# The last matrix of a decode block: other cuts of its transfer, fewer wide products

## The chip, the cores and the metric

The kernel runs on one core of a Trainium2 chip. The metric is the device time of one execution in microseconds; runs are compared by their median. Everything is in float32.

## What is computed

One decode step of a transformer block for a batch of four tokens: an adaptive layer norm conditioned on `c`, attention over a window of 2048 cached positions (32 query heads, 8 key and value heads), a second adaptive layer norm, and a gated feed-forward net. The change touches the last product of the feed-forward net alone. Its part of the reference:

```python
def _B_ref(x, w1, w3, w2):
    gate = jnp.einsum("bsd,df->bsf", x, w1)
    up = jnp.einsum("bsd,df->bsf", x, w3)
    h = _silu(gate) * up
    out = jnp.einsum("bsf,fd->bsd", h, w2)
    return out

...
h = _layernorm(x, axis=-1) * (1 + cb) + sb
x = x + gb * _B_ref(h, B_w1, B_w3, B_w2)
```

`w1` and `w3` are 512 x 1792, `w2` is 1792 x 512, and there are four tokens.

## The kernel before

The kernel reads about 100 MB once and in a fixed order: modulation weights, `wq`, the key and value blocks of eight groups, `wo`, `w1`, `w3`, `w2`. All of it goes through one large tile, `ring`, whose parts are loaded again when their last reader is done. SyncE issues nearly all of the transfers. The program is written out as one list of operations; `Program` works out the waits from the tiles that the operations touch. Each engine carries out its own operations in the order of the list. `do.mark()` splits the list in two parts with semaphores of their own: when all engines have passed the mark, GpSimd clears the semaphores of the first part.

The feed-forward net ends the kernel. `ffn_in` (line 431) multiplies the normed tokens `h2T` with `w1`, then with `w3`, into `s_ps[0]` and `s_ps[1]`; ScalarE copies the result out, TensorE transposes it, and VectorE makes the hidden values, `hidT` (line 459). `hidT` holds 14 chunks of 128 hidden features, and `w2` has 14 chunks of 128 rows by 512 columns to match (256 KB a chunk).

`w2` is loaded at line 412 in four pieces, one transfer each, cut at `W2_CUTS`, which counts chunks: 8, 3, 2 and 1. The transfers are issued one behind another on SyncE's queue, behind that of `w3`. A product waits for the piece that holds its columns.

Two forms of product are used for a chunk:

- **Wide** (lines 466 to 468): one product of 512 columns for a chunk, into one of four strips of 32 partitions of `part` (`s_ps[3]`). Four chunks go to four strips, the next four are added to them. So each strip ends as a partial sum over its own chunks, and the four strips have to be added together. ScalarE copies `part` to `work` (line 469), and TensorE adds the strips by a product of `work` with `sames`, a matrix of ones and zeros.
- **Narrow** (`add_rows`, line 471): eight products of 64 columns for a chunk, one for each of four strips `j` and two halves `s`. They put the output into `y_ps` (`s_ps[2]`) in its final place: strip `j` holds columns `j * 128` to `j * 128 + 127`, and the two halves `s` of these lie in different rows of the strip. No addition of strips is needed. `add_rows(sames, work, ...)` takes the partial sums of the wide products into `y_ps` by the same route.

A float32 product appears as two matmul instructions in the profile, each with a weight load of its own.

The order on TensorE's queue is: chunks 0 to 7 wide; chunks 8, 9, 10 narrow; `sames` by `work`; chunks 11 and 12 narrow; the mark; chunk 13 narrow. VectorE then multiplies `y_ps` with the gate and adds the residual (lines 484 and 485), and SyncE writes the result out (line 486). The input layout on the host (`_layout`, line 490) puts the weights in the order in which the chunks are read; `edge` holds the last two chunks.

Of the kernel before, what the change touches and what calls it, by code (L numbers as in the profile page):

```python
# [8 lines left out]
B, D, HQ, G, SK, DH, W, FF = 4, 512, 32, 8, 8192, 128, 2048, 1792  # L9
P = 128  # L10
# [2 lines left out]
NC = 4  # L13
NF = FF // P
BLOCK = FF // 4
W2_CUTS = [0, 8, 11, 13, 14]
GUESTS = 240
GUEST_AT = [(0, 0, 12), (12, 0, 12), (24, 0, 8), (64, 0, 12), (76, 0, 12), (84, 4, 12)]
EPS = 1e-5
# [128 lines left out]
def block_kernel(nc, w_mod_a, wq, guests, kv_in, wo_mod, last_k_wo, last_v, wo, w1, w3, w2, out):  # L148
# [5 lines left out]
    do = Program(nc)  # L154

    def sb(name, *shape):
        return nc.alloc_sbuf_tensor(name, (P, *shape), F32).ap()
# [16 lines left out]
    def load(dst, src, cuts=(0, 1), queue="sync"):  # L174
        step = src.shape[1] // cuts[-1]
        for lo, hi in zip(cuts[:-1], cuts[1:]):
            do(queue, "dma_start", dst[:, lo * step : hi * step], src[:, lo * step : hi * step])
        return dst[:, : src.shape[1]]
# [7 lines left out]
    first = load(slots[0], w_mod_a)  # L186
# [22 lines left out]
    hidT = sb("hidT", NF, 36)  # L209
# [11 lines left out]
    sames = sb("same", 36)  # L221
# [83 lines left out]
    work = sb("work", 512)  # L305
    for half in range(2):
        qp = s_ps[half]
        for k in range(4):
            for i in range(4):
                at = ((half * 4 + i) * 4 + k) * 512  # L310
                n = min(512, 16384 - GUESTS - at)
# [28 lines left out]
    def heads_out(g):  # L340

        otp = bank()[:, : R * B]
        if g < G - 1:
            do("tensor", "matmul", otp, o_sum, pick, start=True, stop=True)
        else:
            for c in range(NC):
                do("tensor", "matmul", otp, work[:, c * P : (c + 1) * P], pick_c[:, c].rearrange("p r b -> p (r b)"), start=(c == 0), stop=(c == NC - 1))
        do("vector", "tensor_copy", oT[:, g].rearrange("p r b -> p (r b)"), otp)
# [49 lines left out]
    last = k_wo[:, :HALF], load(ring[:, 2 * HALF : 3 * HALF], last_v)  # L398
# [12 lines left out]
    w3_t = load(slots[0][:, HALF:], w3)  # L411
    w2_t = load(slots[0][:, :HALF], w2, W2_CUTS)
    heads_out(G - 1)
# [14 lines left out]
    H = P // 2  # L428
# [33 lines left out]
    y_ps, y, res = s_ps[2][:, :H], p_sb[2][:, :H], p_sb[3][:, :H]  # L462

    part = s_ps[3]
    w2_t = w2_t.rearrange("p (n c) -> p n c", n=NF)
    for n in range(W2_CUTS[1]):
        i = n % 4
        do("tensor", "matmul", part[32 * i : 32 * i + 32, :], hidT[:, n, 4:], w2_t[:, n, :], start=(n < 4), stop=(n + 4 >= W2_CUTS[1]))
    do("scalar", "copy", work, part)

    def add_rows(rows, columns, start, stop):
        for s in range(2):
            for j in range(4):
                at = j * P + s * H
                do("tensor", "matmul", y_ps[32 * j : 32 * j + 32, :], rows[:, 4 - 4 * s : 36 - 4 * s], columns[:, at : at + H], start=(start and s == 0), stop=(stop and s == 1))

    for n in range(W2_CUTS[1], NF):
        if n == W2_CUTS[-2]:
            do.mark()
        if n == W2_CUTS[2]:  # L480

            add_rows(sames, work, False, False)
        add_rows(hidT[:, n], w2_t[:, n], n == W2_CUTS[1], n == NF - 1)
    do("vector", "tensor_mul", y, y_ps, halves[:, 0])
    do("vector", "tensor_add", res, y, halves[:, 1])
    do("sync", "dma_start", out, res)
# [3 lines left out]
def _layout(i):  # L490
    import numpy as np

    def a(t):
        return np.ascontiguousarray(t)

    k = i["A_k_cache"][:, :, SK - W :, :].reshape(B, G, NT, 512, DH)
    v = i["A_v_cache"][:, :, SK - W :, :].reshape(B, G, NT, NC, P, DH)
    wm = i["w_mod"].reshape(4, P, 6, 4, P)
    xc = np.concatenate([i[n].reshape(B, 4, P).transpose(2, 1, 0).reshape(P, 16) for n in ("A_x", "c")], 1)
    w2 = i["B_w2"].reshape(4, BLOCK, D)  # L500
    edge = w2[:, 3 * P :].reshape(2, 2, P // 2, D).transpose(1, 0, 2, 3).reshape(2, P, D)
    w2 = np.concatenate([w2[:, : 3 * P].reshape(4, 3, P, D).transpose(1, 0, 2, 3).reshape(12, P, D), edge])
    wq = a(i["A_wq"].reshape(4, P, G, 512).transpose(1, 2, 0, 3)).reshape(P, 16384)
    guests = np.zeros((2, 12, 6, GUESTS), np.float32)
    for n, (at, lo, hi) in enumerate(GUEST_AT):
        for m in range(2):
            guests[m, lo:hi, n] = wq[at + 32 * m + lo : at + 32 * m + hi, 16384 - GUESTS :]
    wo = a(i["A_wo"].reshape(2, 4, R, P, D).transpose(0, 3, 1, 2, 4)).reshape(2, P, 8192)
    kv = np.concatenate([k.transpose(1, 4, 2, 0, 3).reshape(G, P, 8192), v.transpose(1, 4, 2, 0, 3, 5).reshape(G, P, 8192)], 2)
    return {  # L510
        "w_mod_a": np.concatenate([a(wm[:, :, :2].transpose(1, 0, 3, 2, 4)).reshape(P, 4096), xc], 1),
        "wq": a(wq[:, : 16384 - GUESTS]),
        "guests": guests.reshape(24, 6 * GUESTS),
        "kv_in": kv[: G - 1],
        "wo_mod": np.concatenate([wo[0], a(wm[:, :, 2:].transpose(1, 0, 3, 2, 4)).reshape(P, 8192)], 1),
        "last_k_wo": np.concatenate([kv[G - 1, :, :8192], wo[1, :, :4096]], 1),
        "last_v": a(kv[G - 1, :, 8192:]),
        "wo": a(wo[1, :, 4096:]),
        "w1": a(i["B_w1"].reshape(4, P, FF).transpose(1, 0, 2)).reshape(P, 4 * FF),
        "w3": a(i["B_w3"].reshape(4, P, FF).transpose(1, 0, 2)).reshape(P, 4 * FF),  # L520
        "w2": a(w2.transpose(1, 0, 2)).reshape(P, NF * D),
    }
# [15 lines left out]
```

## Time and profile before

| what | value |
|---|---|
| median of 3 runs | 242.5 us (242.18 to 242.52) |
| the profiled execution | 242.21 us |
| its span, first to last instruction | 240.8 us |
| bytes moved by DMA | 101.39 MB, mean 421 GB/s over the span |
| TensorE matmul busy | 147.8 us, 61% of the span |
| mean granted TensorE clock | 0.865 |
| chain that ended last: DMA, TensorE, VectorE, ScalarE | 60%, 31%, 5%, 3% |

The span is what the profiler shows between the first and the last instruction of the program; the execution's own time contains 1.4 us more around it. "PE" in the rows is TensorE with its products, "PEld" are its weight loads, which run beside the products. A row of a timeline shows the start, the length, the engine, the operation with output and inputs, the number of instructions merged into the row, and, in brackets, how long the engine sat idle before and what it waited for. The products are pipelined and their ends are modelled, so overlapping products of four strips appear as one busy stretch. In the rows of transfers the last number is the time from the issue to the landing, that is until the waiting engine may go on; it contains the queueing behind everything issued earlier.

All parts of the tile `s_ps` have one name in the profile, and all pieces of `w1`, `w3` and `w2` appear as `ring<-w`; they are told apart by size and by order. Every operation is recorded by a helper at line 59, so rows are told apart by tile and shape.

### The profile page before, as it was taken

The page shows a single profiled execution, that of the slowest core. Times are in us where ns is not written, and L with a number is a line of the kernel's source. Part 1 is how long each engine was busy: PE and PEld are TensorE (multiplying, and loading weights), DVE is VectorE, ACT ScalarE, POOL GpSimd, SP SyncE. Part 2 cuts the span into 40 slices and gives each one's busy share as a digit, 9 for nine tenths or more (in the row PEclk, how much of TensorE's full clock was granted, in tenths as well). Part 3 has the DMA queues.
Part 4 walks back from the last instruction along what each step waited for, and adds up shares of the span by engine and source line. Part 5 has one row for each costly group of instructions (what it writes and reads, how often), then busy time and mean ns, then how long its engine had stood idle before and what let it go on. Part 6 is the DMA issues. An engine that isn't in the chain of part 4 may idle for free.

```text
span 240.8 us, 2490 instructions
## 1 busy us (share of the span) xinstructions
PE 147.8 (61%) x1109; PEld 53.2 (22%) x1109; DVE 55.1 (23%) x138; ACT 23.9 (10%) x36; POOL 4.5 (2%) x12
## 2 busy tenths in 40 slices
PE   0000169982984962944867576567489719964866
PEld 0000133322222212201311122221042202422323
DVE  5000231034152024123132133130313104103110
ACT  2000000003003003001100300300210000320100
POOL 7000000000000000000000000000000000000000
PEclk9999997997696798879797799795759968996899
DMA  8999999999999999999999999999999999999994
GB/s 316 434 442 442 430 425 446 427 436 436 436 414 449 414 448 414 449 425 446 425 446 427 436 436 436 436 416 457 403 468 416 403 419 436 406 431 443 403 414 163
DMA packets 2937, 101.39 MB, mean 421 GB/s; under 512 B 472, under 2 KB 472, under 8 KB 880
## 3 DMA queue, kind: packets, MB, share of 16 engines
q1 hardware_dynamic: 2784, 92.99, 89.8%
q10 hardware_dynamic: 144, 8.27, 8.0%
q8 instruction: 8, 0.13, 0.2%
q14 instruction: 1, 0.01, 0.0%
HBM read 101.22 MB, written 0.03 MB: 421 GB/s over the span
## 4 chain that ended last, share of the span: by engine, by line
DMA 60%; PE 31%; DVE 5%; ACT 3%; issue 1%; ACTq 0%
DMA ring<-kv_in 33%; DMA ring<-w 16%; PE s_ps L59 14%; DMA ring<-w_mod_a 11%; PE bank L59 9%; PE o_ps L59 6%; DVE nm L59 3%; ACT p_sb L59 3%; PE a_ps L59 1%; DVE mod_a L59 0%; ACT work L59 0%; DVE p_sb L59 0%; DVE e L59 0%; DVE h L59 0%; DVE sq L59 0%
## 5 line engine op out<-in xcount | busy, mean ns | idle before, releaser
L59 PE MATMUL s_ps<-ring,qT 128*32 128x512 f32 x256 | 36.5, 722 | 20.3 <-DMA ring<-kv_in 13.3
L59 PE MATMUL bank<-ident,p_sb 128*128 128x128 f32 (+1 forms) x142 | 28.1, 349 | 31.7 <-ACT p_sb L59 31.6
L59 PE MATMUL o_ps<-ring,pT 128*16 128x512 f32 x256 | 38.6, 709 | 0.1
L59 PEld LDWEIGHTS bank<-ident,p_sb 128*128 128x128 f32 (+1 forms) x142 | 19.9, 176 | 55.2 <-ACT p_sb L59 34.6
L59 ACT ACTIVATE p_sb<-s_ps,nm 128x2048 f32<-128x2048 f32 (+1 forms) x11 | 16.5, 1501 | 139.8 <-DVE oT L59 104.2
L59 DVE TENSOR_REDUCE nm<-s_ps 128x1 f32<-128x2048 f32 x7 | 16.0, 2292 | 32.6 <-PE s_ps L59 32.6
L59 DVE COPY pT<-bank 128x64 f32<-128x64 f32 x32 | 7.2, 225 | 57.1 <-PE bank L59 57.1
L59 PEld LDWEIGHTS s_ps<-ring,qT 128*32 128x32 f32 x256 | 8.7, 129 | 47.0 <-issue 20.1
L59 PE MATMUL bank<-ident,xs 128*128 128x128 f32 x1 | 0.5, 477 | 27.9 <-POOL xs L59 27.9
L59 PE MATMUL s_ps<-ring,hT 128*32 128x512 f32 (+1 forms) x64 | 9.4, 705 | 0.1
L59 PE MATMUL s_ps<-ring,h2T 128*32 128x448 f32 x64 | 8.2, 662 | 2.0 <-DMA ring<-w 2.0
L59 PEld LDWEIGHTS o_ps<-ring,pT 128*16 128x16 f32 x256 | 5.4, 100 | 11.8 <-issue 9.0
L59 DVE SCALAR_TENSOR_TENSOR o_own<-o_ps,rl,own 128x512 f32<-128x512 f32 x7 | 5.3, 751 | 11.1 <-PE o_ps L59 11.1
L59 PE MATMUL a_ps<-ring,oT 128*4 128x512 f32 x64 | 7.4, 592 | 0.0
L59 DVE TENSOR_REDUCE o_sum<-o_own 128x128 f32<-128x512 f32 x7 | 7.2, 1032 | 0.2
L59 PE MATMUL bank<-ring,sc 128*32 128x256 f32 (+1 forms) x64 | 6.9, 584 | 0.0
L59 PEld LDWEIGHTS bank<-ident,xs 128*128 128x128 f32 x1 | 0.2, 183 | 27.9 <-POOL xs L59 27.9
L59 DVE TENSOR_SCALAR e<-e 128x16 f32<-128x16 f32 x1 | 0.2, 175 | 23.4 <-ACT e L59 23.4
L59 DVE COPY qT<-bank 128x64 f32<-128x64 f32 x8 | 2.2, 279 | 12.6 <-PE bank L59 12.2
L59 DVE TENSOR_REDUCE mx<-s_ps 128x1 f32<-128x512 f32 x4 | 2.8, 692 | 9.0 <-PE s_ps L59 9.0
L59 PE MATMUL s_ps<-ring,hidT 128*32 128x64 f32 (+1 forms) x112 | 3.7, 276 | 0.4 <-DVE hidT L59 0.4
L59 PEld LDWEIGHTS s_ps<-ring,h2T 128*32 128x32 f32 x64 | 2.3, 131 | 6.7 <-issue 4.2
(94 smaller groups left out, 60.7 us busy)
## 6 DMA issues: line engine op xcount, KB each, us to landing
ring<-wq ACTq DMA_DIRECT2D x1, 8072.0 KB, 27.0
ring<-w SPq DMA_DIRECT2D x2, 3584.0 KB, 38.0
ring<-last_k_wo SPq DMA_DIRECT2D x1, 6144.0 KB, 30.1
ring<-last_v SPq DMA_DIRECT2D x1, 4096.0 KB, 39.5
ring<-w_mod_a SPq DMA_DIRECT2D x1, 2064.0 KB, 26.8
ring<-wo SPq DMA_DIRECT2D x1, 2048.0 KB, 41.8
ring<-w SPq DMA_DIRECT2D x1, 2048.0 KB, 43.1
ring<-w SPq DMA_DIRECT2D x1, 768.0 KB, 44.5
```

The costliest lines, as they stand in the source:

```text
L59: op = Op(engine, lambda: getattr(getattr(self.nc, engine), method)(*args, **kw), [])
```

## The change

`w2` is cut at half chunks: the four pieces hold 8, 4, 1.5 and 0.5 chunks. Only chunks 0 to 3 are wide products; chunks 4 to 13 are narrow. The product of `sames` with `work` stands ahead of chunk 8, the first of the second piece, instead of ahead of chunk 11. The last chunk is laid out by halves: its columns for `s` = 0 come first and belong to the third piece, and those for `s` = 1 are the fourth piece. The mark moves between the two halves of the last chunk.

```diff
-W2_CUTS = [0, 8, 11, 13, 14]
+W2_CUTS = [0, 16, 24, 27, 28]
+WIDE, SUMS = 4, 8
...
-    for n in range(W2_CUTS[1]):
+    for n in range(WIDE):
         i = n % 4
-        do("tensor", "matmul", part[32 * i : 32 * i + 32, :], hidT[:, n, 4:], w2_t[:, n, :], start=(n < 4), stop=(n + 4 >= W2_CUTS[1]))
+        do("tensor", "matmul", part[32 * i : 32 * i + 32, :], hidT[:, n, 4:], w2_t[:, n, :], start=(n < 4), stop=(n + 4 >= WIDE))
     do("scalar", "copy", work, part)
 
-    def add_rows(rows, columns, start, stop):
+    def add_rows(rows, columns, first=False, last=False):
         for s in range(2):
+            if last and s == 1:
+                do.mark()
             for j in range(4):
-                at = j * P + s * H
-                do("tensor", "matmul", y_ps[32 * j : 32 * j + 32, :], rows[:, 4 - 4 * s : 36 - 4 * s], columns[:, at : at + H], start=(start and s == 0), stop=(stop and s == 1))
-
-    for n in range(W2_CUTS[1], NF):
-        if n == W2_CUTS[-2]:
-            do.mark()
-        if n == W2_CUTS[2]:
-
-            add_rows(sames, work, False, False)
-        add_rows(hidT[:, n], w2_t[:, n], n == W2_CUTS[1], n == NF - 1)
+                at = s * 4 * H + j * H if last else j * P + s * H
+                do("tensor", "matmul", y_ps[32 * j : 32 * j + 32, :], rows[:, 4 - 4 * s : 36 - 4 * s], columns[:, at : at + H], start=(first and s == 0), stop=(last and s == 1))
+
+    for n in range(WIDE, NF):
+        if n == SUMS:
+            add_rows(sames, work)
+        add_rows(hidT[:, n], w2_t[:, n], n == WIDE, n == NF - 1)
...
     edge = w2[:, 3 * P :].reshape(2, 2, P // 2, D).transpose(1, 0, 2, 3).reshape(2, P, D)
+    edge[1] = edge[1].reshape(P, 4, 2, P // 2).transpose(0, 2, 1, 3).reshape(P, D)
```

## The prediction

> **What bounds the kernel now.** I read the chain of work that ended last first, in its last stretch. Columns: start in us, length in us, engine or transfer, tile.
>
> ```profile
> 191.02 38.54 DMA ring<-w
> ...
> 234.33 0.27 DVE hidT L59
> 234.59 0.04 issue
> 234.64 2.62 PE s_ps L59 x64
> 237.26 0.01 issue
> 237.27 1.46 PE s_ps L59 x64
> 238.73 0.02 issue
> 238.75 0.23 DVE p_sb L59
> ```
>
> Up to 229.56 the end hangs on the transfer of w3. Nothing of the change lies ahead of `hidT` (234.59), and the first w2 piece is 8 chunks in both kernels, so the whole question lies between 234.6 and 238.75, where VectorE starts on the sum. The chain gives that stretch to PE alone. It can't be taken at its word: it follows the modelled ends of products, and a short wait for a transfer vanishes under the 0.2 us in which earlier products drain. So next I read the DMA issues with their time to landing, and SyncE's timeline for the moment of each issue. First the four issues of w2 in order, then their landings (KB, us from issue to landing).
>
> ```profile
> 191.39 0.43 SPq L59 DMA_DIRECT2D ring<-w  x1
> 191.87 0.43 SPq L59 DMA_DIRECT2D ring<-w  x1
> 192.34 0.43 SPq L59 DMA_DIRECT2D ring<-w  x1
> 192.82 0.45 SPq L59 DMA_DIRECT2D ring<-w  x1
> ...
> ring<-w SPq DMA_DIRECT2D x1, 2048.0 KB, 43.1
> ring<-w SPq DMA_DIRECT2D x1, 768.0 KB, 44.5
> ring<-w SPq DMA_DIRECT2D x1, 512.0 KB, 45.2
> ring<-w SPq DMA_DIRECT2D x1, 256.0 KB, 45.4
> ```
>
> Issue plus time to landing: chunks 0-7 are there at 234.49, 8-10 at 236.37, 11-12 at 237.54, 13 at 238.22. Against that the weight loads of the stretch. They start where a product really could be issued, so they show the waits that the chain hides.
>
> ```profile
> 234.64 0.16 PEld L59 LDWEIGHTS s_ps<-ring,hidT 128*32 128x32 f32 x8 [0.49 <-DVE hidT L59]
> 235.09 0.13 PEld L59 LDWEIGHTS s_ps<-ring,hidT 128*32 128x32 f32 x4 [0.30 <-issue]
> 235.52 0.13 PEld L59 LDWEIGHTS s_ps<-ring,hidT 128*32 128x32 f32 x4 [0.30 <-issue]
> 236.38 0.72 PEld L59 LDWEIGHTS s_ps<-ring,hidT 128*32 128x32 f32 x48 [0.73 <-DMA ring<-w]
> 236.63 0.58 ACT L59 COPY work<-s_ps 128x512 f32<-128x512 f32 x1 [3.21 <-PE s_ps L59]
> 237.26 0.27 PEld L59 LDWEIGHTS s_ps<-work,same 128*32 128x32 f32 x16 [0.17 <-ACT work L59]
> 237.63 0.49 PEld L59 LDWEIGHTS s_ps<-ring,hidT 128*32 128x32 f32 x32
> 238.25 0.27 PEld L59 LDWEIGHTS s_ps<-ring,hidT 128*32 128x32 f32 x16
> 235.95 1.31 PE L59 MATMUL s_ps<-ring,hidT 128*32 128x512 f32 x52
> ```
>
> A product in f32 is two instructions here. The wide chunks 0-7 go in four rounds, at 234.64, 235.09, 235.52 and 235.95 (the last row's start): 0.43 to 0.45 us a round of two chunks. Chunks 8-10 start at 236.38, their piece having landed at 236.37. `sames` waits for ScalarE's copy: 237.10 to 237.26, a stall of 0.16. Chunk 11 starts at 237.63, 0.09 after its piece landed, and chunk 13 at 238.25, 0.03 after its own. So the last landing, 238.22, sets the end; then come one chunk of 16 pairs and the drain, until VectorE starts at 238.75, 0.50 after the chunk's start.
>
> **The change part by part.** *Price of a narrow chunk.* Sixteen load-and-product pairs take 0.27, 32 take 0.49, 48 take 0.72: each 16 more cost 0.22 to 0.23, or 0.014 us a pair. *Price of a wide chunk*: half a round, 0.22. They agree, since 16 pairs of 64 columns and 2 of 512 stream the same number of columns. So turning chunks 4-7 from wide to narrow (8 wide instructions out, 64 narrow pairs in, counted against each other) adds 4 x 0.22 and takes away 2 x 0.44: nothing, within 0.05. The granted clock is full throughout, so the prices can be added:
>
> ```profile
> 234.60:237.30 2.70, 2.66 (x68) 1.17 (x70) 0.00 (x0) 0.58 (x1) 0.00 (x0) 1.00 0.90 355
> 237.30:238.80 1.50, 1.38 (x64) 1.00 (x64) 0.05 (x1) 0.00 (x0) 0.00 (x0) 1.00 0.08 31
> ```
>
> (columns: length, busy and count of PE, PEld, VectorE, ScalarE, GpSimd, granted clock, DMA share, GB/s).
>
> The Trainium skill's page "TensorE: Matmul & The Clock Gate", section "Wait — 56ns, not 53.3ns?", says that starts of products never come closer than about 25 ns, however narrow; by that rule a narrow chunk would cost 0.40 us and this change would be a loss. The trace disagrees at 0.014 us a pair, four column strips at once, for runs of up to 48 pairs; it is a rival below for longer runs.
>
> *The landings.* Six chunks between the first and last landing take 238.22 - 234.49 = 3.73 us, 0.62 a chunk (single steps: 0.63, 0.59, 0.68, with no sign of a cost per piece). Four pieces stay four pieces, with the same issues on SP at 0.43 to 0.45 us each, behind which SP has nothing until the output. The second piece, now 4 chunks, lands at 234.49 + 4 x 0.62 = 236.97; the third, 1.5 chunks, at 237.90; the last at 238.22 as before. From both sides: the last two pieces get shorter rows, which the trace doesn't show. If the half-chunk piece took as long as the 256 KB one now (0.68), it would land at 238.58; if it landed at its share of the fastest step (0.30), at 238.20. I take 238.22, next to the even steps.
>
> The Trainium skill's "DMA: Bandwidth & Descriptors", section "Anatomy of one DMA — SWDGE (gpsimd) path", gives about 2.0 us a transfer plus its bytes, and speaks against small ones; by it a last piece alone behind the third would take some 2.3 us. Here a 256 KB piece landed 0.68 us behind its forerunner, so queued pieces don't show that charge.
>
> *The new sequence.* Two wide rounds: 234.64 to 235.52. ScalarE's copy began 0.68 after the start of the last round (235.95 to 236.63); now that round starts at 235.09, so the copy runs from 235.77 to 236.35. ScalarE had been idle for 3.21 us, and nothing is queued ahead of it. Chunks 4-7: 64 pairs, 0.90, until 236.42. `sames` then waits for the copy with chunks 8-13 queued behind it on PE; the copy was ready 0.07 earlier, and were it later, the wait for the second piece covers another 0.3. `sames`: 0.22, until 236.64. So the 0.16 stall goes, but PE now waits for the second piece, until 237.00. Chunks 8-11: 0.90, until 237.90. The third piece is there, wait included, at 237.94. Chunk 12 and the first half of 13, 24 pairs: 0.36 (16 take 0.27, 8 more 0.11, less the start's share), until 238.30. The last piece has been there since 238.22. The last 8 pairs: 0.11, until 238.41. Before, 16 pairs from 238.25 ended at 238.47 (16 x 0.014), and VectorE began 0.28 later; now it begins at 238.69. The gain is 0.06 us; at most 0.11 if PE is ready for the last piece when it lands. The rest of the advantage is eaten by the third piece: PE gets 24 pairs to do 0.3 us before the last landing, where before it had done 32 pairs and stood waiting from 238.12.
>
> *The rest.* The relaid last chunk is done in the input layout and costs no instruction. The mark moves half a chunk later: behind it each engine adds to a semaphore and GpSimd clears the first part's. GpSimd's work there must only end before 240.8, 2.5 us later; I cost it at nothing, and it would count only beyond that cover. The output's two VectorE operations and its transfer stay.
>
> Sum: 242.21 (the profiled execution: span 240.8 and 1.4 around it) - 0.06 = 242.15. That execution is 0.29 below the median of the runs, 242.5; from the median the same step gives 242.4, which I forecast, a change of under 0.05%. The measurement of this kernel can tell about 0.2%, some 0.5 us, from no change.
>
> **Rivals.**
>
> *PE isn't fed (slower).* Sixteen pairs stand where two did, so the program is longer by 56 products and 56 loads, and PE's instructions come through DMA too:
>
> ```profile
> q8 instruction: 8, 0.13, 0.2%
> ...
> q8 instruction: 1, 0.02, 5.2%
> ...
> 212.25:236.19 23.94, 16.62 (x135) 0.86 0.99 419
> 236.19:240.80 4.61, 2.49 (x116) 1.00 0.23 86
> ```
>
> The first row is the whole run's (8 blocks of 16 KB), the second that of the window 236.1 to 237.4: one block, 5.2% of 16 engines over 1.3 us, so 1.08 us long. The third and fourth count PE's products from the seventh block to the eighth (135) and from there to the end (116). With 56 more behind it, a ninth block falls due in the last 40 or so products, at about 237.7 to 238.3. For: that is the tail itself, and a block that PE needs at once would hold it for about 1.1 us, less 0.1 of slack: 243.2 to 243.4. Against: while the eighth came, from 236.38 on, PE issued 48 pairs without a gap, so blocks come ahead of need. It decides only if fewer than 1.1 / 0.014, some 80 pairs, are in hand when a block is asked for. The Trainium skill's "Runtime: NRT & Kernel Launch", section "Instruction fetch mechanics", has such 16 KiB blocks fetched ahead and mostly hidden. Chance 0.04.
>
> *Long narrow runs slow down (slower).* No run of before exceeds 48 pairs; now 80 stand in one row and 64 behind. A run's first 16 pairs cost 0.27, or 0.017 a pair; were all 176 narrow pairs from 235.52 on at that, they would end at 238.51, 0.1 late. The rival tells from 0.019 us a pair on: they end at 238.86, 0.45 late, which is 242.9 from the median, and each further 0.001 adds 0.18. Against: 0.014 held evenly from 16 to 48 pairs. By the Trainium skill's rule of 25 ns, weighed above, the end would be 1.5 late, at 243.9. Chance 0.03.
>
> *The small last piece lands late.* At 238.58 PE would start on it at 238.61 and VectorE at 239.00: 0.25 late, 242.75, still within 0.2%. For: its rows are half the smallest now. Against: steps of 0.59 to 0.68 a chunk whatever the piece. Chance 0.08.
>
> *The landings don't bind (faster).* If all pieces were there in time, as the chain reads, PE would go from 235.52 through 176 pairs, 2.47, to 237.99, and VectorE start at 238.27: 0.48 early, 242.0, just at what can be measured. It needs each piece 0.3 us earlier, with the same bytes. The transfers do end before the landings:
>
> ```profile
> 237.40:237.60 0.20, 0.20 (x16) 0.13 (x12) 0.00 (x0) 0.00 (x0) 0.00 (x0) 1.00 0.28 103
> 237.60:237.80 0.20, 0.20 (x20) 0.17 (x16) 0.00 (x0) 0.00 (x0) 0.00 (x0) 1.00 0.06 21
> ```
>
> so some 0.4 us lie between the last bytes and 238.22; were that to shrink with the piece, this case would come nearer. Chance 0.10.
>
> **How the numbers follow.** Forecast (242.4, itself 242.1 to 242.7 by the spread of the runs shown, 242.18 to 242.52): 0.75; late small piece 0.08, counted as no change; landings that don't bind 0.10, most of it beyond or at 0.2%, so faster 0.09; slow rivals 0.07. That leaves no change 0.84. The range goes from 241.9 (the case without landings, and 0.1 of spread) to 242.9 (the late piece with the spread); the block rival is left out.
>
> **What would show it.** In the changed kernel: 8 wide instructions from about 234.6, ScalarE's copy some 0.86 earlier against `hidT`; no wait for `work` before `sames`; 64 pairs at 0.014 each; a wait of about 0.35 for the second piece; then PE within 0.05 of the third landing; VectorE's first step 4.05 us after the start of the wide products, against 4.11 before. Wrong would be a gap within the narrow runs (PE's supply), a last landing later than 3.75 us after the first piece's, or a change ahead of `hidT`, which I hold to be untouched.

## The result and the profile after

| | before | changed |
|---|---|---|
| median of 7 runs, us | 242.32 (242.05 to 242.52) | 243.06 (242.97 to 243.24) |
| ratio, 95% interval | | 1.0032 (1.0021 to 1.0044) |
| profiled execution, its span | 242.21, 240.8 | 243.06, 241.7 |

The changed kernel is slower by 0.74 us, where 0.06 to 0.1 us less was forecast and a range up to 242.9 given. Its chain of work, last stretch (start, length, engine or transfer, tile; the helper is now at line 60):

```profile
192.12 45.17 DMA ring<-w
237.28 0.04 issue
237.33 0.86 PE s_ps L60 x45
238.19 0.42 issue
238.61 0.99 PE s_ps L60 x51
239.60 0.02 issue
239.62 0.23 DVE p_sb L60
```

A piece that was not there before stands in it: 0.42 us of "issue" between 45 and 51 narrow products. "Issue" is time in which the engine waited for nothing that the profile shows. The weight loads of the same stretch:

```profile
234.92 0.16 PEld L60 LDWEIGHTS s_ps<-ring,hidT 128*32 128x32 f32 x8 [0.49 <-DVE hidT L60]
235.38 0.13 PEld L60 LDWEIGHTS s_ps<-ring,hidT 128*32 128x32 f32 x4 [0.30 <-issue]
235.81 0.91 PEld L60 LDWEIGHTS s_ps<-ring,hidT 128*32 128x32 f32 x60 [0.30 <-issue]
236.06 0.59 ACT L60 COPY work<-s_ps 128x512 f32<-128x512 f32 x1 [2.35 <-PE s_ps L60]
236.70 0.27 PEld L60 LDWEIGHTS s_ps<-work,same 128*32 128x32 f32 x16
237.32 0.70 PEld L60 LDWEIGHTS s_ps<-ring,hidT 128*32 128x32 f32 x45 [0.36 <-DMA ring<-w]
238.61 0.81 PEld L60 LDWEIGHTS s_ps<-ring,hidT 128*32 128x32 f32 x51 [0.58 <-issue]
```

Everything up to the row of `sames` is as forecast, 0.28 us later on the clock of this execution because `w3` landed later in it. Then PE stops for 0.58 us after 45 of the 64 pairs that belong to the second piece. All of that piece is in the tile (it landed at 237.3), so no transfer of weights explains the place. Nor did a later piece come late. SyncE's timeline has the issues of the third and the fourth piece, the view of transfers the time to landing of the second to the fourth:

```profile
192.60 0.45 SPq L60 DMA_DIRECT2D ring<-w  x1
193.09 0.43 SPq L60 DMA_DIRECT2D ring<-w  x1
```

```profile
ring<-w SPq DMA_DIRECT2D x1, 1024.0 KB, 45.2
ring<-w SPq DMA_DIRECT2D x1, 384.0 KB, 45.6
ring<-w SPq DMA_DIRECT2D x1, 128.0 KB, 45.4
```

The third and fourth landed at 238.20 and 238.49, 0.29 apart; the second, issued at 192.12 by the chain, at 237.3. What is left is PE's own program. First the page's count of instruction blocks (8 before), then the view of transfers for the windows 236.2 to 236.5 and 239.6 to 239.8:

```profile
q8 instruction: 9, 0.15, 0.2%
```

```profile
q8 instruction: 1, 0.02, 22.3%
...
q8 instruction: 1, 0.02, 29.9%
```

One block of TensorE's program began to move in each of these two windows, about 1.1 and 1.0 us long (22.3% of 16 engines over 0.3 us, 29.9% over 0.2 us). The first was over by 237.4, some 1.3 us before PE went on at 238.61. The second began to move at 239.7, after the pause.

### The profile page after: what moved, and what is told of

The parts are those of the page before. It is cut to its first block, busy times and chain, and to the rows that moved or that the text cites. A ratio compares the mean times of both kernels' runs of the same rounds, so it can differ in the third digit from the quotient of the medians.

```text
span 241.7 us, 2602 instructions
## 1 busy us (share of the span) xinstructions
PE 149.8 (62%) x1165; PEld 54.6 (23%) x1165; DVE 55.2 (23%) x138; ACT 24.0 (10%) x36; POOL 4.5 (2%) x12
## 4 chain that ended last, share of the span: by engine, by line
DMA 63%; PE 28%; DVE 5%; ACT 3%; issue 1%; SPq 0%; ACTq 0%
DMA ring<-w 19%; DMA ring<-kv_in 17%; DMA ring<-wo_mod 16%; PE s_ps L60 12%; DMA ring<-w_mod_a 11%; PE bank L60 9%; PE o_ps L60 6%; DVE nm L60 3%; ACT p_sb L60 3%; PE a_ps L60 1%; SPq L60 0%; DVE mod_a L60 0%; ACT work L60 0%; DVE p_sb L60 0%; DVE e L60 0%
## 5 line engine op out<-in xcount | busy, mean ns | idle before, releaser
L60 PE MATMUL s_ps<-ring,qT 128*32 128x512 f32 x256 | 37.3, 736 | 18.8 <-DMA ring<-kv_in 11.8
L60 PE MATMUL o_ps<-ring,pT 128*16 128x512 f32 x256 | 37.2, 686 | 0.0
L60 PEld LDWEIGHTS bank<-ident,p_sb 128*128 128x128 f32 (+1 forms) x142 | 20.5, 180 | 54.0 <-ACT p_sb L60 34.8
L60 PE MATMUL s_ps<-ring,hT 128*32 128x512 f32 (+1 forms) x64 | 10.3, 764 | 0.0
L60 PE MATMUL s_ps<-ring,h2T 128*32 128x448 f32 x64 | 8.8, 710 | 0.8 <-DMA ring<-w 0.4
L60 PEld LDWEIGHTS s_ps<-ring,hT 128*32 128x32 f32 x64 | 2.5, 137 | 6.9 <-issue 6.8
```

The source lines that it names most:

```text
L60: op = Op(engine, lambda: getattr(getattr(self.nc, engine), method)(*args, **kw), [])
```

## The experiments

Three theories:

- **A**: PE stopped at the border of a 16 KB block of its program, because the next block wasn't there yet. This needs that a block is asked for one block ahead, as PE passes the border before.
- **B**: a long row of narrow products stalls by itself.
- **C**: the new cuts of `w2` cost something.

By A the border is a place in the program, so it can be moved with instructions that do nothing useful and stand far ahead. The padding used is a product of one column with 32 weights, two load-and-product pairs each, written to a PSUM bank that is free at that time. Where it stands behind the third attention group, PE idles for the next key block anyway. The edit, with `N` products:

```diff
     for g in range(G - 1):
         group(g)
+        if g == 2:
+            for n in range(N):
+                do("tensor", "matmul", banks[0][32 * (n % 4) : 32 * (n % 4) + 32, :1], same, ident[:, :1], start=True, stop=True)
```

### 16 pairs of padding (N = 8)

> The changed kernel with 8 more tiny products (16 load-and-product pairs, 64 bytes of program each for 32 instructions, 2 KB) on TensorE after the third attention group, where it idles for the next key block; their result is not used. Theory A (the pause is PE waiting for its next 16 KB block of program): every block border moves 16 pairs earlier in the program; the border inside the wide products falls among the transposes before hidT, so its block is asked for over 0.5 us earlier and is there in time. The 0.6 us pause after 45 of the last 96 narrow pairs goes; VectorE starts on the sum 4.05 to 4.15 us after the first wide product instead of 4.70; time 242.2 to 242.5, about equal to the kernel before. Theory B (a long row of narrow products stalls by itself): pause and time as in the changed kernel, 243.06. Theory C (the new cuts: a late piece): as in the changed kernel, 243.06.

242.02 us, ratio to before 0.9994 (0.9985 to 1.0003). The weight loads:

```profile
234.59 0.16 PEld L60 LDWEIGHTS s_ps<-ring,hidT 128*32 128x32 f32 x8 [0.49 <-DVE hidT L60]
...
236.37 0.27 PEld L60 LDWEIGHTS s_ps<-work,same 128*32 128x32 f32 x16
236.95 1.43 PEld L60 LDWEIGHTS s_ps<-ring,hidT 128*32 128x32 f32 x96 [0.32 <-DMA ring<-w]
238.61 0.22 DVE L60 TENSOR_TENSOR p_sb<-s_ps,xs 128x64 f32<-128x64 f32 x1 [4.07 <-PE s_ps L60]
```

The 96 pairs go out in one row, 1.43 us, 0.015 a pair, with the third and the fourth piece landing meanwhile. VectorE starts 4.02 us after the first wide product; in the changed kernel it was 4.70, before 4.11. With 32 instructions more the program takes some 0.9 us less (the ratio to before went from 1.0032 to 0.9994). B and C expected the pause to stay. It is gone from a row of 96, so B falls.

### 128 pairs (N = 64), one whole block

> As the first, with 64 tiny products, 128 pairs or 256 instructions, just one block of 16 KB. Theory A: all borders come round to where they were, so the pause after about 45 of the 96 pairs is back at its 0.6 us and the time at 243.0 to 243.2. If the padding itself cost time or helped in another way, 242.3 as with 16 pairs, or more than 243.3. Theories B and C: 243.06 too, so this run tells only beside the first.

244.99 us, ratio 1.0115 (1.0102 to 1.0129).

```profile
237.18 0.70 PEld L60 LDWEIGHTS s_ps<-ring,hidT 128*32 128x32 f32 x45 [0.32 <-DMA ring<-w]
239.99 1.42 PEld L60 LDWEIGHTS s_ps<-ring,hidT 128*32 128x32 f32 x51 [2.11 <-issue]
```

The pause is back, and at the same pair: after 45 of 96. So the period is 128 pairs. Its length was missed: 2.11 us, not 0.6. By the view of transfers the block began to move only between 237.5 and 238.0 here; in the changed kernel it was between 236.2 and 236.5.

The pause isn't the whole loss. The 51 pairs behind it took 1.42 us, in the changed kernel 0.81. The view by windows, for the weight loads (length, busy and count, granted clock, DMA share, GB/s):

```profile
240.20:241.40 1.20, 1.20 (x43) 0.50 0.00 0
```

The granted clock is 0.50 here; in the changed kernel it is 1.00 over its 51 pairs. So the clock dropped just behind the longest pause, and that adds 0.6 us. In the other paused profiles the granted clock stays at 1.00 through the tail.

### 4 pairs (N = 2)

> As the first, with 2 tiny products, 4 pairs. Theory A: the border lies 4 pairs earlier, so the pause comes after 41 of the last 96 pairs instead of 45, and the border in the wide products comes at their very start, 0.1 to 0.4 us earlier: a pause of 0.3 to 0.6 us, time 242.8 to 243.1. Theories B and C: after 45 pairs, 0.6 us, 243.06.

243.29 us, ratio 1.0047 (1.0033 to 1.0061).

```profile
234.60 0.16 PEld L60 LDWEIGHTS s_ps<-ring,hidT 128*32 128x32 f32 x8 [0.49 <-DVE hidT L60]
...
236.96 0.64 PEld L60 LDWEIGHTS s_ps<-ring,hidT 128*32 128x32 f32 x41 [0.31 <-DMA ring<-w]
238.53 0.82 PEld L60 LDWEIGHTS s_ps<-ring,hidT 128*32 128x32 f32 x55 [0.93 <-issue]
```

Four pairs earlier in the program, and the pause is four pairs earlier: after 41. It is longer than expected (0.93 against 0.3 to 0.6).

### Half the change: four wide chunks with the old cuts

> One part of the change alone: chunks 0 to 3 wide, 4 to 13 narrow, the sum of the strips ahead of chunk 8, but the pieces of before (8, 3, 2, 1 chunks), the old layout of the last chunk and the mark ahead of it. Theory A: as many instructions as in the changed kernel, so the same border and a pause after about 45 of the last 96 pairs (now inside chunk 10), ending about 3.7 us after the first wide product; then 51 pairs, 0.7 us: time 242.9 to 243.2. Theory B: also a pause. Theory C (the cuts did it): no pause, 242.2 to 242.5.

```diff
-W2_CUTS = [0, 16, 24, 27, 28]
+W2_CUTS = [0, 8, 11, 13, 14]
 WIDE, SUMS = 4, 8
```

(with the old layout of the last chunk and the mark ahead of it.) 244.26 us, ratio 1.0086 (1.0072 to 1.0099), above the expected 243.2.

```profile
236.56 0.73 PEld L60 LDWEIGHTS s_ps<-ring,hidT 128*32 128x32 f32 x45
238.94 0.81 PEld L60 LDWEIGHTS s_ps<-ring,hidT 128*32 128x32 f32 x51 [1.65 <-issue]
239.95 0.22 DVE L60 TENSOR_TENSOR p_sb<-s_ps,xs 128x64 f32<-128x64 f32 x1 [5.41 <-PE s_ps L60]
...
240.46 0.34 SPq L60 DMA_DIRECT2D out<-p_sb  x1
```

The old cuts, and the pause after 45 of 96 pairs again: C falls. The pairs reach the border earlier here, because the second piece lands earlier, and wait longer. The rest of the excess lies behind the sum. The output took 2.7 us to land, in the changed kernel 1.6, and in the window 240.5 to 241.0 another block began to move:

```profile
out<-p_sb SPq DMA_DIRECT2D x1, 32.0 KB, 2.7
```

```profile
q8 instruction: 1, 0.02, 14.4%
```

That the output's share on one DMA engine stood behind that block fits both rows, but wasn't tested by itself.

### The other half: the new cuts with eight wide chunks

> The other part of the change alone: the new cuts, the new layout of the last chunk and the mark between its halves, but chunks 0 to 7 wide as before and the sum of the strips behind chunk 11 (ahead of the third piece). Theory A: TensorE's program is as long as in the kernel before, the next block border lies 5 pairs behind the last product, so no pause; by the rows of the forecast VectorE starts on the sum 4.2 us after the first wide product (4.11 before), time 242.2 to 242.4. Theory C (the new cuts themselves cost): 242.8 or more.

```diff
 W2_CUTS = [0, 16, 24, 27, 28]
-WIDE, SUMS = 4, 8
+WIDE, SUMS = 8, 12
```

242.34 us, ratio 1.0005 (0.9996 to 1.0015). No pause; VectorE started 4.20 us after the first wide product (234.81 to 239.01), as worked out. So the cuts cost nothing that can be measured, and the loss belongs to the narrow products' instructions.

### The kernel before with 12 pairs more in its tail

> The kernel before with 6 tiny products (12 pairs, result not used) between chunk 10 and the sum of the strips, where PE waits 0.16 us for ScalarE anyway: 12 x 0.014 = 0.17 us of issue. Theory A: the border that lies 5 pairs behind the last product now lies 7 pairs ahead of it, inside the last chunk; its block is asked for at the second wide round, 0.4 us after the first, and comes 3.0 to 4.7 us later (the spread of the runs so far), while PE gets there 3.75 us after the first wide product. So a pause of 0 to 1.3 us after 9 of the last chunk's 16 pairs, time 242.2 to 243.6, likeliest 242.6 to 243.0, and up to 1.2 us more if the block after that stands in front of the output's transfer. Theory B or C: no pause, 242.2 to 242.4.

```diff
+            for m in range(6):
+                do("tensor", "matmul", banks[0][32 * (m % 4) : 32 * (m % 4) + 32, :1], same, ident[:, :1], start=True, stop=True)
             add_rows(sames, work, False, False)
```

242.24 us, ratio 1.0003 (0.9994 to 1.0011). That is the low end of what A allowed and not its likeliest, 242.6 to 243.0. By the time alone the run doesn't tell the theories apart. The weight loads of the last chunk, from two windows that part the row, show more:

```profile
238.33 0.19 PEld L59 LDWEIGHTS s_ps<-ring,hidT 128*32 128x32 f32 x9
...
238.49 0.15 PEld L59 LDWEIGHTS s_ps<-ring,hidT 128*32 128x32 f32 x7
```

Behind the ninth of the last 16 pairs, the place that A named, the next load starts 0.08 us after the one before it (238.41 to 238.49), where the chunk in the kernel before has steps of at most 0.04. The block's packet was over at 237.0. In the paused runs PE went on 1.26 to 1.42 us after that (the table below), which would be 238.3 to 238.5 here; PE came to the border at 238.4, about as the block came to be of use. No ninth block moved in this run, though PE passed the border with 7 pairs to go.

### 8 pairs (N = 4)

> The changed kernel with 4 tiny products, 8 pairs, after the third attention group. Theory A: the border in the wide products moves just ahead of them, among the transposes that precede hidT, so its block is asked for about 0.5 us before the first wide product: a pause after 37 of the last 96 pairs, shorter by some 0.5 us than with 4 pairs (0.93 there): 0 to 0.7 us; time 242.2 to 242.8, between those with 4 and 16 pairs. Any theory without the program's length: 243.06.

242.04 us, ratio 0.9996 (0.9987 to 1.0004): no pause, 96 pairs in one row of 1.46 us. The step from 4 pairs (243.29) to 8 pairs (242.04) is a step in when the block came: it began to move at 236.06 with 4 pairs and at 233.39 with 8, long before PE got to it. A expected this, because the border one block ahead slips from behind the wait for `hidT` to ahead of it. The exact place doesn't fit: 128 pairs ahead of the pause would lie behind the fourth of the seven transposes, which start at 233.47, and the block moved before that. So here the block was asked for at least four pairs earlier than 128 ahead; how many stays open.

### 16 pairs behind the last product

> The changed kernel with the 8 tiny products of the first experiment placed behind the last product of the sum instead of ahead of it. Theory A: the border ahead of it doesn't move, so the pause stays at 45 of the last 96 pairs, and the time is that of the changed kernel or, with no more than 0.2 us, above it: 243.0 to 243.4. If a longer program or the tiny products themselves did the good in the first experiment: 242.0 to 242.3.

The eight products of the first experiment stand behind the last `add_rows` instead. 243.22 us, ratio 1.0042 (1.0029 to 1.0054), with the pause after 45 pairs (0.74 us). A longer program as such does no good; the padding helps only ahead of the border.

### 256 pairs (N = 128)

> The changed kernel with 128 tiny products, 256 pairs, two whole blocks of 16 KB, after the third attention group (some 4 us of issue in a gap of PE). Theory A: the borders come round a second time, the pause is after 45 of the last 96 pairs once more; it lasts until the block is there, 3.4 to 4.7 us after it was asked for in the runs so far, so 0.6 to 2.2 us, time 243.0 to 245.0. If the 2.1 us with 128 pairs grew with the padding and not with the block's own wait: a pause of 3 us or more, 246. Theories B and C: 0.6 us.

244.64 us, ratio 1.0101 (1.0084 to 1.0118). The pause is after 45 of 96 pairs for the third time, 0.49 us long, so its length doesn't grow with the padding. The time isn't the pause's alone: in this run everything in the tail came later, from the landing of `w3` on (the first wide product at 236.06 instead of 234.6 to 234.9; with 112 pairs, below, it is at 235.50). All four executions with this padding took 244.15 us or more, so it probably brought this about; how wasn't followed up.

### 112 pairs (N = 56)

> The changed kernel with 56 tiny products, 112 pairs, that is 16 pairs short of a whole block. Theory A: every border lies 16 pairs further on than in the changed kernel; the one in the wide products moves to 13 pairs into the narrow ones, so its block is asked for 0.5 to 0.6 us later, and the pause comes after 61 of the last 96 pairs, 0.2 us later: longer by some 0.3 us than in the changed kernel at the same wait for the block, 0.9 to 2.3 us, time 243.3 to 245.3. Theories B and C: after 45 pairs, 0.6 us, 243.06.

244.43 us, ratio 1.0098 (1.0077 to 1.0120).

```profile
237.47 0.95 PEld L60 LDWEIGHTS s_ps<-ring,hidT 128*32 128x32 f32 x61
239.55 0.59 PEld L60 LDWEIGHTS s_ps<-ring,hidT 128*32 128x32 f32 x35 [1.14 <-issue]
```

A border 16 pairs further on, and the pause is 16 pairs further on, after 61, 1.14 us long. Here the span ends at 242.3, but the profiled execution took 245.4 us, 3.1 more instead of 1.4. A block of instructions moved behind the span's end (the window 242.3 to 246.0):

```profile
q8 instruction: 1, 0.02, 2.5%
```

So an execution may last until a block that was asked for has come, even one that holds nothing it still needs. This is read from one profile and wasn't tested; the other three executions took 244.27 to 244.45, some 1.6 more than their spans.

## Why the prediction was wrong

| kernel | pause after pair, of 96 | its length, us | block moved, us | PE went on after its end, us | VectorE after first wide, us | median, us |
|---|---|---|---|---|---|---|
| before | none | | 236.19 to 237.27 | | 4.11 | 242.32 |
| changed | 45 | 0.58 | 236.28 to 237.35 | 1.26 | 4.70 | 243.06 |
| + 4 pairs | 41 | 0.93 | 236.06 to 237.15 | 1.38 | 4.97 | 243.29 |
| + 8 pairs | none | | 233.39 to 234.41 | | 4.02 | 242.04 |
| + 16 pairs | none | | 233.66 to 234.75 | | 4.02 | 242.02 |
| + 16 pairs at the end | 45 | 0.74 | 235.98 to 237.11 | 1.29 | 4.80 | 243.22 |
| + 112 pairs | 61 | 1.14 | 237.19 to 238.21 | 1.34 | 4.84 | 244.43 |
| + 128 pairs | 45 | 2.11 | 237.55 to 238.65 | 1.34 | 6.88 | 244.99 |
| + 256 pairs | 45 | 0.49 | 237.14 to 238.23 | 1.38 | 4.56 | 244.64 |
| wide 4, old cuts | 45 | 1.65 | 236.45 to 237.52 | 1.42 | 5.36 | 244.26 |
| wide 8, new cuts | none | | 235.99 to 237.25 | | 4.20 | 242.34 |

"Block moved" is the packet of the last block of TensorE's program that began to move before the place of the pause, read from the traces. In all seven runs with a pause PE goes on 1.26 to 1.42 us after that packet's end, wherever the pause stands and however long it is. That ties the end of the pause to the block. When the block was asked for is not in the profile. That it is asked for at one border and needed at the next is inferred: it goes with the period of 128 pairs, and with the 2.7 us by which four pairs moved the block. It isn't exact, as the runs with 8 pairs and with 12 in the tail of before show.

**The bound and the chain.** Right: the tail from `hidT` on decided, and nothing ahead of it changed but by the scatter of single executions.

**The prices.** Right. Two wide rounds took 0.89 (0.88 worked out), the copy began 1.14 after the first wide product (1.13), there was no wait for `work` ahead of `sames`, PE waited for the second piece until 2.40 after the start (2.36), and narrow pairs cost 0.015 us in rows of 60 and 96 (0.014). The Trainium skill's rule of 25 ns between starts ("TensorE: Matmul & The Clock Gate", "Wait — 56ns, not 53.3ns?") would put 96 pairs at 2.4 us; the 16-pair run shows 1.43 with four strips at once.

**The landings.** Right: the small last piece wasn't late, and "landings that don't bind" didn't come about. The 2.0 us a transfer that the prediction takes from the Trainium skill stand there, by the title of the section, for transfers that GpSimd issues; these are SyncE's, so they are no test of it.

**The sum.** Right for a kernel in which PE is fed in time: with 8 or 16 pairs of padding VectorE starts at 4.02, where 4.05 was worked out, and both medians lie 0.1 to 0.2 us under that of before, in intervals that hold no change. No version here beats the kernel before by what can be measured.

**The step that failed** is the rival "PE isn't fed", given a chance of 0.04. It was named, and with the right mechanism, but its point of decision was mis-sized twice.

- Its price was the length of one block's packet, 1.08 us. The packets took that, but PE went on only 1.26 to 1.42 us after their end, or 2.3 to 2.5 us after their start. Ahead of the start lies the time from asking to moving, which the profile doesn't show. How much of the wait is the weights' doing on the same DMA engines wasn't tried.
- So the point of decision isn't "fewer than 80 pairs in hand". A block holds 128 pairs, which at 0.015 us are 1.9 us of narrow products, less than a block takes from its start to PE's going on.
- The argument against it, that PE issued 48 pairs without a gap while the eighth block came, showed only that PE was working off the block it had. In the kernel before the next border lies some 5 pairs behind the last product (45 + 64 + 16 + 8 = 133 pairs from the first wide one; it has 128), so it never gets there. With 12 pairs more it does, at 238.4, and stops for less than 0.1 us; the changed kernel is there at some 238.0, before the block is of use, and has 51 pairs still to do. I looked for the ninth block in the tail; the one that PE waited for was the eighth, which both profiles show.

By these sizes the change's account is: 0.63 us for the pause (51 pairs begun at 238.61 instead of 237.98 or so), less the 0.06 that the change gains, or 0.57, within the measured interval of 0.51 to 1.07. The median moved by 0.74; the rest isn't accounted for.

The Trainium skill ("Runtime: NRT & Kernel Launch", "Instruction fetch mechanics") describes a program fetched in 16 KiB blocks of 256 instructions, the next while the current one runs, with the cost of a border mostly hidden. The period agrees: 128 pairs are 256 instructions, and 128 more bring the pause back. That it is hidden doesn't hold in this tail: 0.5 to 2.1 us showed.

## What to carry to other kernels

Count the instructions of a stretch as well as its columns: eight 64-column products in place of one of 512 stream the same columns, but with eight times the instructions, and a stretch that runs through 128 load-and-product pairs faster than a block of program can be fetched (here 2.3 to 2.5 us from the start of its transfer, and some time from asking to that start) stops at a border. The sign in the profile is an idle gap put down to "issue", in the middle of a row whose data is all there, and it moves pair by pair with any instruction added ahead. Before judging such a change, move the borders: 8 idle products far ahead turned a loss of 0.3% into no difference, and 64, which bring the borders back, a loss of over 1%.

## What the runs showed of the hardware

- TensorE stopped for 0.5 to 2.1 us at a border in its program, with a period of 128 load-and-product pairs. It went on 1.26 to 1.42 us after the end of a block's packet of about 1.1 us, in seven runs. When the packet starts differs (235.98 to 237.55 us in them); why stays open.
- Behind the longest pause, 2.11 us, the granted clock was 0.50, and 51 pairs took 1.42 us in place of 0.81.
- A block may also disturb others: one moved beside an output that took 2.7 instead of 1.6 us to land, and one behind the end of a span whose execution took 1.7 us longer around it than usual. Neither was tested.
